# A fused Fourier mixer and gated MLP on one core: the last half sum of a seven-product block goes from a DMA to VectorE, the activation's addition and the second layer move one step later, and loads and buffers are rearranged

## The chip, the cores and the metric

The kernel runs on 1 core of one Trainium2 chip. The metric is the device time of one execution in microseconds (us), lower is better. Engines are named as the profile names them: PE is TensorE, PEld its weight loads, DVE is VectorE, ACT is ScalarE, POOL is GpSimd, SP is SyncE. POOL and SP issue the DMAs here.

## The reference

```python
# x (8, 3008, 256), filt_r and filt_i (1505, 256), w_in (256, 2048), w_out (2048, 256), alpha (2048)
X = np.fft.rfft(x, axis=1)
Y = X * (filt_r + 1j * filt_i)[None]
y = np.fft.irfft(Y, n=3008, axis=1).reshape(24064, 256)
h = y @ w_in
g = np.maximum(h, 0.0) + alpha * np.minimum(h, 0.0)
out = (g @ w_out).astype(np.float32)
```

So each of eight batches is filtered along its 3008 rows by a Fourier transform, and each of the 24064 rows then goes through a two-layer MLP with a leaky activation whose slope is given for each of 2048 hidden features.

## The kernel before, in words

**Two streams, one order.** Everything is issued in one hand-written order. The MLP works on 48 blocks of 512 rows (every twelfth, at n = 5 mod 12, has 384), and a block has 16 steps. In step j, `up(j)` multiplies the block's rows with 128 columns of `w_in` (two matmuls, L495). At every odd j the two hidden tiles just made are a pair: ACT copies the pair from PSUM to `gtb` (L503), DVE forms `m = min(g, 0) * (alpha - 1)` in two instructions (L506) and adds it to `g` (L507). The Fourier transform of batch b+1 runs beside the MLP of batch b in pieces named a, b, c, d; the tuples `STEPS_A` to `STEPS_D` (and `FIRST` for batches 1 to 3) say at which step, counted from p = 96(b-1), a piece is issued. `plan` holds these pieces, and each step runs its `plan` entries before `up(j)`.

**The second layer** of a block trails its first layer by `LAG` = 16 steps: after `up(j)`, items (matmuls) of the older block are issued as long as `done < (step - LAG) / 16`. For the 21 block numbers in `FAST`, the second layer is `seven()`: a 2 x 2 split with seven products instead of eight, 112 matmuls of 128 columns (L554), so seven a step. The four quarters of the block's `g` are `a11`, `a21`, `a12`, `a22`; the sums that the seven products need are made in halves h = 0, 1 by `sums(w, h)`:

- w = 1: `z1 = a21 + a22` on DVE (L515); w = 2: `z2 = z1 + a11` on DVE (L517)
- w = 3: `a21 += a11` by an accumulating DMA from POOL's queue (L519, rows `gtb<-gtb`)
- w = 4: `a12 += z2` by an accumulating DMA from POOL's queue (L521, rows `gtb<-ss`); it may start once the first product has read that half of `a12`, and the last product (items 96 to 111; its second half begins at item 104) reads the result

`SUMS` says at which step after a block's first one each sum is issued; `TAIL` does so for blocks 40 and 42 to 45. The other blocks use `eight()` (64 matmuls of 256 columns, L532).

**Around it.** Piece b takes one of two PSUM banks, DVE makes `ww` (L233) and `uu` (L234) from it, and two accumulating DMAs from POOL (L236, rows `uu<-ww`) finish `uu` for piece c (L248). `BANKS` is a string that says which of the two banks each piece gets. `load_x` brings a quarter c of a batch's rows in with two DMAs from POOL, one for each half (L168, `xs`). The results go out from `osb` tiles (pool `p_osb`, three buffers) by DMAs from SP's queue. `late` holds the last additions on DVE (L474) and the stores of a seven-product block, and `flush()` issues them at the start of the next step.

Of the kernel before, what the change touches and what calls it, by code (L numbers as in the profile page):

```python
# [10 lines left out]
FP16 = mybir.dt.float16  # L11
FP32 = mybir.dt.float32

NFFT = 3008
N1 = 47
N2 = 64
NK1 = 24
D = 256
# [2 lines left out]
NH = 32  # L21
BANKS = (
    "010101010101010101010101010101001010010110010010101010101010100101001010010101010101010100101010"
    "101010101010101010101001001010110100101010100101001000101101010101010101101001011101010001010010"
    "101101010011010101101010101010101010110010101010101101001000101001010101010101010101010101010110"
    "101010101011010010010101101010101010101010101010101010011010010101001011011101011010101010101010"
    "10101010101010010101010010110001010101010101010101010101"
)
STEPS_A = (-84, -81, -77, -76, -65, -59, -58, -58, -56, -53, -52, -51, -50, -48, -46, -43)
STEPS_B = (-21, -15, 4, 6, 13, 21, 25, 27, 32, 40, 54, 55)  # L30
# [5 lines left out]
STEPS_F = (20, 16, 22, 28, 34)  # L36
STEPS_K = (118, 121, 128, 133, 144)
STEPS_X = ((20, 27, 42, 52), (107, 109, 113, 126))
FIRST = (
# [12 lines left out]
)  # L52
FAST = frozenset((8, 10, 12, 14, 16, 18, 20, 22, 24, 26, 28, 30, 32, 34, 36, 38, 40, 42, 43, 44, 45))
SUMS = ((9, 1, 0), (10, 3, 0), (16, 2, 0), (17, 1, 1), (17, 3, 1), (19, 2, 1), (20, 4, 0), (21, 4, 1))
TAIL = ((12, 1, 0), (12, 3, 0), (18, 1, 1), (18, 3, 1), (18, 2, 0), (18, 2, 1), (20, 4, 0), (21, 4, 1))
LAG = 16
AF = mybir.ActivationFunctionType
OP = mybir.AluOpType

# [41 lines left out]
def kernel(  # L101
# [10 lines left out]
    nc = tc.nc  # L112
# [9 lines left out]
    konst = ctx.enter_context(tc.tile_pool(name="konst", bufs=1))  # L122
    p_x = ctx.enter_context(tc.tile_pool(name="p_x", bufs=4))
# [3 lines left out]
    p_sn = ctx.enter_context(tc.tile_pool(name="p_sn", bufs=1))  # L127
    p_uw = ctx.enter_context(tc.tile_pool(name="p_uw", bufs=3))
    p_m = ctx.enter_context(tc.tile_pool(name="p_m", bufs=2))
    p_osb = ctx.enter_context(tc.tile_pool(name="p_osb", bufs=3))  # L130
    psH = ctx.enter_context(tc.tile_pool(name="psH", bufs=2, space=bass.MemoryType.PSUM))
    psO = [ctx.enter_context(tc.tile_pool(name=f"psO{i}", bufs=1, space=bass.MemoryType.PSUM)) for i in range(2)]
    psF = [ctx.enter_context(tc.tile_pool(name=f"psF{i}", bufs=1, space=bass.MemoryType.PSUM)) for i in range(2)]
# [9 lines left out]
    twi_s = konst.tile([128, NK1, 128], FP16, name="twi_s")  # L143
    filt_s = konst.tile([128, NK1, D], FP16, name="filt_s")
    filts_s = konst.tile([128, NK1, D], FP16, name="filts_s")
    al16 = konst.tile([16, 128], FP32, name="al16")
    id32 = konst.tile([16, 16], FP32, name="id32")
    al_s = konst.tile([128, 16], FP32, name="al_s")
    alm_s = konst.tile([128, 16], FP32, name="alm_s")
# [11 lines left out]
    def xrow(b, h, c):  # L161
        return bass.AP(tensor=x.tensor, offset=x.offset + (b * NFFT + NH * h + 8 * c) * D,
                       ap=[[N2 * D, N1], [1, 8 * D]])

    def load_x(b, c):
        xs = p_x.tile([2 * N1, 8 * D], FP16, name="xs")
        for h in range(2):
            nc.gpsimd.dma_start(out=xs[h * N1 : h * N1 + N1], in_=xrow(b, h, c))  # L168
        return xs

    def load_filt(dst, pbase, src, ka, kb):
        n = kb - ka
# [181 lines left out]

    nc.sync.dma_start(out=id16, in_=id_d.ap())
    nc.sync.dma_start(out=wfx_s, in_=wfx_d.ap())
    xc = {(0, c): load_x(0, c) for c in range(4)}
    f0 = First()
    nc.sync.dma_start(out=al16, in_=moe_alpha.rearrange("(j p) -> j p", p=128))
    nc.sync.dma_start(out=wf1_s, in_=wf1_d.ap())  # L360
# [71 lines left out]
        for k in range(max(kp - 2, 0), kp - 1) if kp < 8 else (6, 7) if kp == 8 else (kp,):  # L432
            f0.piece_c(k, on_act)
    for c in range(4):
        xc[(1, c)] = load_x(1, c)
    for q in range(2):
        nc.gpsimd.dma_start(
            out=wout_s[:, 8 * q : 8 * q + 8],
            in_=moe_w_out[1024 * q : 1024 * q + 1024].rearrange("(j p) d -> p j d", p=128))
# [32 lines left out]
    def flush():  # L472
        for fn, args in late:
            fn(*args)  # L474
        late.clear()

    class Block:
# [12 lines left out]
        def up(self, j):  # L490
            tn = self.tn
            if j % 2 == 0:
                self.hps = psH.tile([128, 2, 512], FP32, name="hps")
            for kt in range(2):
                nc.tensor.matmul(self.hps[:, j % 2, 0:tn], win_s[:, kt, j * 128 : (j + 1) * 128],  # L495
                                 yT[:, kt, self.t0 : self.t0 + tn], start=(kt == 0), stop=(kt == 1))
            if j % 2 == 1:
                g = self.pair(j // 2)
                m = p_m.tile([128, 2, 512], FP16, name="m")
                hs, ms = self.hps[:, :, 0:tn], m[:, :, 0:tn]  # L500
                if self.fast:
                    hs, ms = (t.rearrange("p l (h c) -> p l h c", h=2) for t in (hs, ms))
                nc.scalar.activation(g, hs, AF.Copy)  # L503
                for i in range(2):
                    a = alm_s[:, j - 1 + i : j + i]
                    nc.vector.tensor_scalar(ms[:, i], g[:, i], 0.0, a, OP.min, OP.mult)  # L506
                nc.vector.tensor_add(g, g, ms)  # L507

        def sums(self, w, h):
            k = slice(4 * h, 4 * h + 4)  # L510
            a11, a21, a12, a22 = (self.q[:, l, t, k] for l in range(2) for t in range(2))
            z1, z2 = ss[:, 0, k], ss[:, 1, k]
            assert w != 4 or self.sent >= 8 * h + 8
            if w == 1:
                nc.vector.tensor_add(z1, a21, a22)  # L515
            elif w == 2:
                nc.vector.tensor_add(z2, z1, a11)  # L517
            elif w == 3:
                nc.gpsimd.dma_start(out=a21, in_=a11, accum_op=OP.add)  # L519
            else:  # L520
                nc.gpsimd.dma_start(out=a12, in_=z2, accum_op=OP.add)  # L521

        def items(self):
            return self.seven() if self.fast else self.eight()
# [87 lines left out]
    def put(step, fn, *args):  # L612
        plan.setdefault(step, []).append((fn, args))
# [17 lines left out]
    for b in range(1, NB):  # L631
        p = 96 * (b - 1)
        f = Fft(b)
        steps_a, steps_b, steps_c, steps_d = FIRST[b - 1] if b < 4 else (STEPS_A, STEPS_B, STEPS_C, STEPS_D)
        for i in range(16):
            put(p + steps_a[i], f.piece_a, i, on_act)
            if i % 4 == 3:
                put(p + steps_a[i] + (b > 2), f.save_a, i // 4)
        if b + 1 < NB:
            for c in range(4):  # L640
                put(STEPS_X[b - 1][c] if b < 3 else p - 8 + 4 * c,
                    lambda b=b, c=c: xc.update({(b + 1, c): load_x(b + 1, c)}))
        quarters, later = (4, 1) if b < 3 else (1, 4)
        w = NK1 // quarters
        for q in range(quarters):
            put(p + steps_a[15] + later, f.turn_a, nc.sync, w * q, w * q + w)
        for kp in range(12):
            put(p + steps_b[kp], f.piece_b, kp)
            put(p + steps_c[kp], f.piece_c, kp, on_act)
            if kp % 3 == 2:  # L650
                put(p + steps_c[kp] + 1, f.turn_c, kp // 3)
        for i in range(16):
            put(p + steps_d[i], f.piece_d, i, on_act)
        put(p + steps_d[3] + 2, f.load_z, 3)
# [15 lines left out]

    for n in range(5):
        put(STEPS_K[n], combine, n)
    blk, todo, ahead = Block(-2, 0, 0, 0), [], {}
    done = 0.0
    for n, (p, t0, tn, _) in enumerate(blocks):
        old, blk = blk, Block(n, p, t0, tn)
        if blk.fast:
            for at, w, h in SUMS if n < 39 and n - 1 not in FAST else TAIL:
                ahead.setdefault(16 * n + at, []).append((blk, w, h))
        for j in range(16):  # L680
            step = 16 * n + j
            flush()
            for b, w, h in ahead.pop(step, ()):
                assert w > 2 or not old.fast or b is old or old.sent >= 88 - 16 * w + 8 * h
                b.sums(w, h)
            for fn, args in plan.pop(step, ()):
                fn(*args)
            blk.up(j)
            while todo and done < (step - LAG) / 16:
                try:  # L690
                    done += next(todo[0])
                except StopIteration:
                    todo.pop(0)
        todo.append(blk.items())
    for it in todo[:-1]:
        for _ in it:
            pass
# [33 lines left out]
```

## Time and profile before

| What | Value |
|---|---|
| Median of 3 runs | 785.37 us (785.03 to 786.56) |
| The profiled execution's own time | 783.02 us |
| Its span, first to last instruction | 780.6 us |
| PE busy | 759.1 us, 97% |
| DVE busy | 687.2 us, 88% |
| ACT busy | 605.3 us, 78% |
| POOL busy | 277.3 us, 36% |
| Granted TensorE clock | 1.000 |

Busy time is time in which the profile shows the engine at an instruction. The ends of matmuls are modelled, so a PE that shows as busy can still run below its peak; its idle times and what ended them are the better guide. A row of the waits gives the engine and line that waited, what it waited for, the sum in us, the number of times, and the longest.

### The profile page before, as it was taken

The page shows a single profiled execution, that of the slowest core. Times are in us where ns is not written, and L with a number is a line of the kernel's source. Part 1 is how long each engine was busy: PE and PEld are TensorE (multiplying, and loading weights), DVE is VectorE, ACT ScalarE, POOL GpSimd, SP SyncE. Part 2 cuts the span into 40 slices and gives each one's busy share as a digit, 9 for nine tenths or more (in the row PEclk, how much of TensorE's full clock was granted, in tenths as well). Part 3 has the DMA queues.
Part 4 walks back from the last instruction along what each step waited for, and adds up shares of the span by engine and source line. Part 5 has one row for each costly group of instructions (what it writes and reads, how often), then busy time and mean ns, then how long its engine had stood idle before and what let it go on. Part 6 is the DMA issues. An engine that isn't in the chain of part 4 may idle for free. (4 is left out here: it accounts for less than half of the span.)

```text
span 780.6 us, 18307 instructions
## 1 busy us (share of the span) xinstructions
PE 759.1 (97%) x6952; PEld 540.0 (69%) x6952; DVE 687.2 (88%) x1501; ACT 605.3 (78%) x902; POOL 277.3 (36%) x367
## 2 busy tenths in 40 slices
PE   7899999999999999999999999999999999999998
PEld 6756667666667767676676766767667777777666
DVE  3788996899999899899898989889899999889994
ACT  3787778788778887788877887788878777787763
POOL 7830651245244351553334423434323434102210
PEclk9999999999999999999999999999999999999999
DMA  9996868667988679975888769886797555735642
GB/s 185 193 198 177 154 123 208 177 135 148 202 193 175 148 145 194 236 148 125 169 213 176 138 135 200 188 173 129 160 201 175 112 113 95 180 84 112 121 96 68
DMA packets 115184, 122.93 MB, mean 157 GB/s; under 512 B 12873, under 2 KB 94553, under 8 KB 115097
## 3 DMA queue, kind: packets, MB, share of 16 engines
q0 software_dynamic: 34960, 52.19, 41.0%
q1 hardware_dynamic: 79992, 69.52, 33.4%
q8 instruction: 54, 0.88, 0.5%
q14 instruction: 34, 0.27, 0.1%
q10 hardware_dynamic: 144, 0.07, 0.0%
HBM read 56.06 MB, written 46.66 MB: 132 GB/s over the span
## 5 line engine op out<-in xcount | busy, mean ns | idle before, releaser
L503 ACT ACTIVATE gtb<-hps 128x1024 f16<-128x1024 f32 (+1 forms) x384 | 386.4, 1006 | 106.9 <-PE hps L495 104.3
L495 PE MATMUL hps<-yT,win_s 128*128 128x512 f16 (+1 forms) x1536 | 449.3, 375 | 0.0
L506 DVE TENSOR_SCALAR m<-gtb,alm_s 128x512 f16<-128x512 f16 (+1 forms) x768 | 235.1, 348 | 52.3 <-ACT gtb L503 50.2
L507 DVE TENSOR_TENSOR gtb<-gtb,m 128x1024 f16<-128x1024 f16 (+1 forms) x384 | 261.5, 681 | 17.2
L532 PE MATMUL op<-wout_s,gtb 128*128 128x256 f16 x1600 | 243.3, 272 | 0.0
L532 PEld LDWEIGHTS <-gtb 128*128 128x128 f16 x1600 | 156.0, 98 | 105.1
L236 POOL DMA_DIRECT2D uu<-ww x168 | 141.7, 1041 | 242.7 <-DVE uu L234 131.2
L495 PEld LDWEIGHTS <-win_s 128*128 128x128 f16 x1536 | 136.6, 98 | 25.7 <-issue 2.6
L554 PEld LDWEIGHTS <-gtb 128*128 128x128 f16 x1680 | 114.4, 98 | 57.4 <-DMA gtb<-ss 5.0
L519 POOL DMA_DIRECT2D gtb<-gtb x42 | 41.5, 987 | 197.8 <-DVE ss L515 75.5
L554 PE MATMUL op<-wout_s,gtb 128*128 128x128 f16 x1008 | 85.8, 219 | 4.1 <-DMA gtb<-ss 3.6
L280 ACT ACTIVATE asb<-psF 96x512 f16<-96x512 f32 x112 | 65.4, 595 | 11.5 <-PE psF L210 10.8
L280 ACT ACTIVATE yT<-psF 128x376 f16<-128x376 f32 x120 | 57.3, 490 | 11.0 <-PE psF L273 10.4
L554 PEld LDWEIGHTS <-ss 128*128 128x128 f16 x672 | 47.1, 98 | 23.3
L554 PE MATMUL op<-tw_s,gtb 128*128 128x128 f16 x672 | 58.2, 219 | 0.1
L554 PE MATMUL op<-tw_s,ss 128*128 128x128 f16 x672 | 58.0, 219 | 0.0
L233 DVE TENSOR_TENSOR ww<-psF,filts_s 128x512 f16<-128x512 f32 x84 | 57.4, 683 | 0.0
L234 DVE TENSOR_TENSOR uu<-psF,filt_s 128x512 f16<-128x512 f32 x84 | 57.1, 679 | 0.0
L280 ACT ACTIVATE v<-psF 128x512 f16<-128x512 f32 x84 | 49.9, 599 | 9.1 <-PE psF L248 8.3
L168 POOL DMA_DIRECT2D xs<-in_x_dram x64 | 43.2, 1054 | 20.9 <-PE psF L210 13.5
L521 POOL DMA_DIRECT2D gtb<-ss x42 | 45.7, 1290 | 3.2 <-PE op L554 0.9
L210 PE MATMUL psF<-xs,wf_s 94*96 94x512 f16 x112 | 41.2, 381 | 1.8 <-DVE yT L283 0.5
(85 smaller groups left out, 518.2 us busy)
## 6 DMA issues: line engine op xcount, KB each, us to landing
out_dram<-osb SPq DMA_DIRECT2D x127, 128.0 KB
xs<-in_x_dram POOLq DMA_DIRECT2D x64, 188.0 KB, 7.0
a_dram<-asb SPq DMA_DIRECT2D x28, 384.0 KB
uu<-ww POOLq DMA_DIRECT2D x168, 64.0 KB, 3.2
v_dram<-v SPq DMA_DIRECT2D x112, 96.0 KB
zt<-v_dram SPq DMA_DIRECT2D x28, 384.0 KB
gtb<-gtb POOLq DMA_DIRECT2D x42, 256.0 KB, 4.2
gtb<-ss POOLq DMA_DIRECT2D x42, 256.0 KB, 6.1
```

The lines of the kernel that those rows point to most:

```text
L168: nc.gpsimd.dma_start(out=xs[h * N1 : h * N1 + N1], in_=xrow(b, h, c))
L233: nc.vector.tensor_mul(ww, px, filts_s[:, 2 * kp : 2 * kp + 2])
L234: nc.vector.tensor_mul(uu, px, filt_s[:, 2 * kp : 2 * kp + 2])
L236: nc.gpsimd.dma_start(out=uu[o : o + 64], in_=ww[64 - o : 128 - o], accum_op=OP.add)
L280: nc.scalar.activation(o, i, AF.Copy)
L495: nc.tensor.matmul(self.hps[:, j % 2, 0:tn], win_s[:, kt, j * 128 : (j + 1) * 128], yT[:, kt, self.t0 : self.t0 + tn], start=(kt == 0), st ...
L503: nc.scalar.activation(g, hs, AF.Copy)
L506: nc.vector.tensor_scalar(ms[:, i], g[:, i], 0.0, a, OP.min, OP.mult)
L507: nc.vector.tensor_add(g, g, ms)
L521: nc.gpsimd.dma_start(out=a12, in_=z2, accum_op=OP.add)
L532: nc.tensor.matmul(op[:, si % 2], self.pair(k // 2)[:, k % 2, 128 * si : 128 * si + 128], wout_s[:, k], start=(k == 0), stop=(k == 15))
L554: nc.tensor.matmul(acc[:, 128 * i : 128 * i + 128], x[:, k, 128 * i : 128 * i + 128], b[:, k], start=first and k + i == 0, stop=k == 7, sk ...
```

## The change

For seven-product blocks that follow `SUMS`, the sum w = 4, h = 1 becomes w = 6: the same addition, `a12 += z2` for the second half, as a DVE instruction at the same step 21 in place of the DMA. `TAIL` keeps its DMAs, and its first two sums move from step 12 to 13. The activation's addition is no longer issued in `up`: it is put into `owed` and issued by `settle()` in the next step, after that step's `flush`, sums and `plan` entries and before its `up`. `LAG` is 17, so the second layer comes a step later against the first. The loads of x for batches 4 to 7 are issued one half quarter at a time at `STEPS_Q`, from step p - 28 to p + 23, where they were issued two halves at a time at p - 8, p - 4, p and p + 4. `p_osb` has four buffers, and `al16` takes its space from one of them. `BANKS` differs in three of its five rows.

```diff
+STEPS_Q = (-28, -18, -8, -3, 1, 9, 15, 23)
...
-SUMS = ((9, 1, 0), (10, 3, 0), (16, 2, 0), (17, 1, 1), (17, 3, 1), (19, 2, 1), (20, 4, 0), (21, 4, 1))
-TAIL = ((12, 1, 0), (12, 3, 0), (18, 1, 1), (18, 3, 1), (18, 2, 0), (18, 2, 1), (20, 4, 0), (21, 4, 1))
-LAG = 16
+SUMS = ((9, 1, 0), (10, 3, 0), (16, 2, 0), (17, 1, 1), (17, 3, 1), (19, 2, 1), (20, 4, 0), (21, 6, 1))
+TAIL = ((13, 1, 0), (13, 3, 0), (18, 1, 1), (18, 3, 1), (18, 2, 0), (18, 2, 1), (20, 4, 0), (21, 4, 1))
+LAG = 17
...
-    p_osb = ctx.enter_context(tc.tile_pool(name="p_osb", bufs=3))
+    p_osb = ctx.enter_context(tc.tile_pool(name="p_osb", bufs=4))
...
-    al16 = konst.tile([16, 128], FP32, name="al16")
+    al16 = p_osb.tile([128, 2, D], FP32, name="osb")[0:16, 0, 0:128]
...
-    def load_x(b, c):
-        xs = p_x.tile([2 * N1, 8 * D], FP16, name="xs")
-        for h in range(2):
-            nc.gpsimd.dma_start(out=xs[h * N1 : h * N1 + N1], in_=xrow(b, h, c))
-        return xs
+    def load_x(b, c, halves=(0, 1)):
+        if 0 in halves:
+            xc[(b, c)] = p_x.tile([2 * N1, 8 * D], FP16, name="xs")
+        for h in halves:
+            nc.gpsimd.dma_start(out=xc[(b, c)][h * N1 : h * N1 + N1], in_=xrow(b, h, c))
...
-                nc.vector.tensor_add(g, g, ms)
+                owed.append((g, ms))
...
-            elif w == 3:
-                nc.gpsimd.dma_start(out=a21, in_=a11, accum_op=OP.add)
             else:
-                nc.gpsimd.dma_start(out=a12, in_=z2, accum_op=OP.add)
+                a, z = (a21, a11) if w % 2 else (a12, z2)
+                if w < 5:
+                    nc.gpsimd.dma_start(out=a, in_=z, accum_op=OP.add)
+                else:
+                    nc.vector.tensor_add(a, a, z)
...
-                put(STEPS_X[b - 1][c] if b < 3 else p - 8 + 4 * c,
-                    lambda b=b, c=c: xc.update({(b + 1, c): load_x(b + 1, c)}))
+                if b < 3:
+                    put(STEPS_X[b - 1][c], load_x, b + 1, c)
+                else:
+                    for h in range(2):
+                        put(p + STEPS_Q[2 * c + h], load_x, b + 1, c, (h,))
...
+    owed = []
+
+    def settle():
+        for g, ms in owed:
+            nc.vector.tensor_add(g, g, ms)
+        owed.clear()
+
...
             for fn, args in plan.pop(step, ()):
                 fn(*args)
+            settle()
             blk.up(j)
...
         todo.append(blk.items())
+    settle()
```

More of the change, by code (lines that the diff above doesn't have):

```diff
@@ L23 @@
     "010101010101010101010101010101001010010110010010101010101010100101001010010101010101010100101010"
-    "101010101010101010101001001010110100101010100101001000101101010101010101101001011101010001010010"
+    "101010101010101010101001010101001011010101011010110110101101010101010101101001011010101101010010"
     "101101010011010101101010101010101010110010101010101101001000101001010101010101010101010101010110"
-    "101010101011010010010101101010101010101010101010101010011010010101001011011101011010101010101010"
-    "10101010101010010101010010110001010101010101010101010101"
+    "101010101011010010010101101010101010101010101010101010010101101010110100100010100101010101010101"
+    "01010101010101101010101101001110101010101010101010101010"
 )
@@ L356 @@
     nc.sync.dma_start(out=wfx_s, in_=wfx_d.ap())
-    xc = {(0, c): load_x(0, c) for c in range(4)}
+    xc = {}
+    for c in range(4):
+        load_x(0, c)
     f0 = First()
@@ L434 @@
     for c in range(4):
-        xc[(1, c)] = load_x(1, c)
+        load_x(1, c)
     for q in range(2):
@@ L512, in sums @@
             z1, z2 = ss[:, 0, k], ss[:, 1, k]
-            assert w != 4 or self.sent >= 8 * h + 8
+            assert w not in (4, 6) or self.sent >= 8 * h + 8
             if w == 1:
@@ L684 @@
                 assert w > 2 or not old.fast or b is old or old.sent >= 88 - 16 * w + 8 * h
+                assert not (owed and b is blk and h == (j - 1) // 8)
                 b.sums(w, h)
```

## The prediction

> **What bounds the kernel now.** I read the page first, then the waits of PE and of its weight loads, then the same waits in short windows, and last the busy time of DVE for every two blocks. From the page:
>
> ```profile
> span 780.6 us, 18307 instructions
> PE 759.1 (97%) x6952; PEld 540.0 (69%) x6952; DVE 687.2 (88%) x1501; ACT 605.3 (78%) x902; POOL 277.3 (36%) x367
> ```
>
> PE is the bound: it stands idle for 780.6 - 759.1 = 21.5 us, and the change takes no matmul away. So all that it can win is in those 21.5 us (much of it before the first block begins at 37.5 us, and behind the last), and all that it can lose is new idle time of PE. Next, who ended PE's idle times (rows: waiter, what for, us in total, times, longest):
>
> ```profile
> PEld L554 <- DMA gtb<-ss: 5.0, 6, 1.4
> ...
> PEld L248 <- DMA uu<-ww: 2.6, 3, 1.1
> ...
> PEld L351 <- DVE uu L234: 0.9, 1, 0.9
> ...
> PEld L554 <- DVE gtb L507: 0.5, 2, 0.3
> ...
> PEld L554 <- DMA gtb<-gtb: 0.3, 1, 0.3
> ```
>
> The largest row is the last product of a seven-product block, which waits for the accumulating DMA into `a12`, the very DMA whose second half the change removes. I asked for the same rows in windows: 1.1 us in two waits from 215 to 232 us (block 10; the longer is 0.6), 0.9 in one from 314 to 331 (block 16), 1.4 in one from 405 to 420 (block 22), 1.0 in one from 500 to 512 (block 28), and 0.6 in one from 700 to 765 (block 43). Counting the 112 L554 matmuls of each block, PE stands at item 96 (half h = 0) for 0.6 in block 10 and 0.9 in block 16, and at item 104 (h = 1) for 0.5 in block 10, 1.4, 1.0 and the 0.6 of block 43. The 0.3 on `gtb<-gtb` is in block 10, the 0.5 on L507 in blocks 43 and 45. Why blocks 10, 16, 22 and 28? They are those with piece b at their steps 11 and 17 (p - 21 and p - 15). The timeline of POOL in block 28:
>
> ```profile
> 500.18 0.98 POOL L519 DMA_DIRECT2D gtb<-gtb  x1 [3.52 <-DVE ss L515]
> 501.38 1.66 POOL L236 DMA_DIRECT2D uu<-ww  x2 [0.22 <-issue]
> 502.44 2.54 POOL L521 DMA_DIRECT2D gtb<-ss  x2
> 503.62 5.27 POOL L168 DMA_DIRECT2D xs<-in_x_dram  x7
> ```
>
> POOL is in order: L521 stands behind L519, which waits for DVE's `z1`, and behind two `uu<-ww`, which wait for DVE's `ww` and `uu`. The issue comes 3.0 us after the matmuls of step 20 began (499.41), in blocks without that piece 0.5 us after. In block 28 that leaves 5.8 us to item 96 and 7.1 to item 104; L521 lands in 4.1 to 8.9 us, median 6.1. Last, DVE for each two blocks (columns: window, its length, DVE busy and instructions, clock, DMA share, GB/s):
>
> ```profile
> 480.40:510.20 29.80, 26.10 (x61) 1.00 0.95 207
> ...
> 632.20:661.40 29.20, 28.45 (x65) 1.00 0.57 109
> ...
> sum 575.10, DVE 528.18; mean DVE 27.80
> ```
>
> The mean window is 575.1 / 19 = 30.3 us, so DVE has 2.5 us free in it, but only 0.75 from 632 to 661 us, and that is no more than the pauses of 45 ns (17.2 us over 384) ahead of its 16 additions L507.
>
> **The change part by part.** Durations are of the profiled execution; its span is 780.6, its own time 783.02, which is 2.35 below the median of 785.37 that I forecast against. A step takes (768.9 - 37.5) / 768 = 0.95 us.
>
> *Second half sum on DVE.* 16 of the 21 seven-product blocks follow `SUMS`, so 16 DMAs leave POOL's queue and 16 additions of 128x1024 fp16 join DVE's. A sum of the same shape takes 0.685 us (L515, 28.8 / 42): 16 x 0.685 = 11.0 us more for DVE. It must wait until PE has sent 16 items, but DVE gets there later by itself: in block 28 item 16 ended at 499.3, while `z2`, which stands ahead of the sum, ended at 502.5. Behind it are the next pair's L506 and L507, read ten steps later, so nothing waits on it where DVE has room. It ends ten steps ahead of item 104: the waits there in blocks 10, 22 and 28 go, -2.9.
>
> *Second layer a step later (LAG).* Items 96 and 104 move 0.95 us away from the sums. Does the DMA for h = 0 move with them, since it must wait for item 8? No: in block 16 item 8 ended at 311.0 and the issue was at 315.4; in the tail, 703.6 against 707.1. So the 0.6 and 0.9 on h = 0, the 0.6 of block 43 and the 0.3 on `gtb<-gtb` are covered: -2.4. In block 16 the cover is 0.95 for 0.9, so I leave 0.3 of these waits in. At the start, step 17 loses four matmuls of 256 columns (0.44 us by the chain of waits) with which PE could fill waits for ACT: between 0 and +0.44, taken as +0.2, since PE there waits partly and partly not. At the end the last blocks have one step more of old items ahead of them: 0.
>
> *Addition a step later.* The order of DVE's instructions shows that 304 of the 384 additions still stand directly behind their own L506; 80 are passed: 33 by `ww` and `uu` (0.68 each), 15 by `z2` alone, 21 by one last addition of a seven-product block, 11 by others. Where nothing passes, LAG gives the reader 0.95 us more; where `z2` passes pair 7 of a fast block, 0.95 - 0.68 = +0.27 is left, and where `ww` and `uu` pass pair 7 (blocks 19, 25, 31, 37), 0.95 - 1.36 = -0.41 against a distance from that L507's end to PE's read of 1.6, 1.8, 1.2 and 1.3 us: enough. The smallest distances before are 0.05 to 0.25 us (blocks 16, 43, 45, 10, 40, 44) and become larger; the 0.5 on L507 goes: -0.5.
>
> *DVE's added load.* At 2.5 us free it costs nothing. From 601 to 661 us the additions of blocks 36 and 38, perhaps 34, fall where DVE has nothing free, and push all behind them by up to 3 x 0.685 = 2.0 us, against 0.95 us from LAG. Between 0 and +2.0; I take +0.7, one sum, as the distances of blocks 35 to 39 (0.9 to 2.5 us) cover the rest.
>
> *Loads of x.* The same 64 DMAs. POOL has 503.3 us free; no PE wait names `xs` after the first blocks. The eight loads jammed behind L521 held each other up (landing 7.0 to 10.8 us instead of 4.4 to 6.2), but not the sums ahead of them: h = 0 of block 28 landed in 4.53 with them, h = 1 of block 24 in 7.68 without. So their going is worth 0; up to -0.5 if they did slow the sums. What they now stand ahead of is a rival below.
>
> *Fourth result buffer, `al16`, `BANKS`.* ACT waits 0.4 us for a store and PE for none: 0. PE's waits on the two banks are under 5 us in sum, most of it before 92 us; a new order may win or lose 0.5: 0. Stores stand one step later in SP's queue, so some `v` and `zt` transfers go ahead of them; no PE wait names these: 0. The 1.6 us that L248 waits for `uu<-ww` at 486 us stays (its steps do not move), between -1.6 and 0.
>
> Sum: -2.9 - 2.4 - 0.5 + 0.3 + 0.2 + 0.7 = -4.6 us, so 785.4 - 4.6 = **780.8 us**, the profiled span near 776.0.
>
> **The rivals.**
>
> *No gain.* Only the waits at item 104 outside the tail go (-2.9); item 96 still waits because L521 lands late by more than a step gives (its landing varies by 4.8 us), DVE's load costs its full 2.0 and the start its 0.44: 784.9. Against it: the waits at item 96 are all under 0.95.
>
> *DVE becomes the bound (slower).* In 632 to 661 us it already is without free time. If that holds wherever the sums are added, PE waits for L507 by all of 11.0 us: 785.4 - 4.6 - 0.7 + 11.0 = 791.1. It decides where free time in two blocks is below 0.685 us. For it: 75% and more of the additions stay where they were, so the pauses of 45 ns stay too. Against it: 2.5 us are free in the mean.
>
> *Loads of x ahead of `uu<-ww`.* One half now goes out at p + 23, two steps before piece b at p + 25, in the same queue. A `uu<-ww` that was issued some 2.1 us behind two halves (at 168.9 and 169.5) landed in 5.5 and 6.0 us; piece c had 7.4, 6.0, 6.2 and 5.6 us from that issue in batches 3 to 6. At 6.0 that is 0.4 us once: 781.2. At the 7.8 us of the slow row at 222.9 it is 0.4 + 1.8 + 1.6 + 2.2 = 6.0: 786.8. The Trainium skill ("DMA: Bandwidth & Descriptors", "Queues, rings and completion order") says that on each DMA engine the descriptors of a ring are taken in ring order; by that rule it is what stands ahead that delays, which speaks for this rival, and against any gain from taking the loads away behind the sums. The 4.53 us of block 28 agree.
>
> **How the numbers follow.** The forecast has 0.62 (its own range 777 to 783.8). More than that, with the 1.6 at L248 and 0.5 each from loads and banks gone too and no new cost, 776.5 or below: 0.06. No gain 0.12, all of it within 0.2%. DVE as the bound 0.12, slower. The loads ahead of `uu<-ww` 0.08, shared 0.02, 0.03, 0.03 over faster, same and slower. A measurement of this kernel can tell about 0.2% (1.6 us) from no change, so faster is 0.70, same 0.15, slower 0.15. The range of 776.5 to 787.0 takes in the second end of the loads and the no-gain case; it leaves out DVE as the bound and half of the best case, with a little of each edge: under 0.2.
>
> **What would show it.** Right: no PEld wait on `gtb<-ss` from 180 to 660 us, or under 0.5 us in sum; 16 DVE additions `gtb<-gtb,ss` near 0.685 us; 26 rows `gtb<-ss`; DVE near 698 us busy; PE idle near 17 us. Wrong: rows PEld L554 or L532 waiting for DVE's addition by over 2 us, above all from 600 to 690 us (DVE the bound); L248 waiting for `uu<-ww` near 355, 450 and 540 us (loads ahead); a longer stretch before 90 us.

## The result, and the profile after

The changed kernel takes 778.88 us (median of 4 runs, 778.49 to 781.17) against 785.2 us of the kernel before (4 runs, 782.83 to 786.56): a ratio of 0.9937, 95% interval 0.9911 to 0.9963. By the medians it is faster by 6.3 us where 4.6 were forecast; by the ratio it is 4.9 us, and the interval spans 2.9 to 7.0. The profiled execution took 778.49 us.

The page after, first its head:

```profile
span 776.7 us, 18287 instructions
PE 759.6 (98%) x6952; PEld 541.9 (70%) x6952; DVE 691.0 (89%) x1517; ACT 606.1 (78%) x902; POOL 264.7 (34%) x351
```

PE's idle time fell from 21.5 to 17.1 us with the same 6952 matmuls. The span fell by only 3.9 us, less than the medians: the first matmul of step 0 began at 38.8 us here and at 37.5 before. That is not the change: `late_spread` below has the same start and begins it at 37.2; in this execution the granted clock was 0.91 from 20 to 40 us, before it was 1.00. From the first to the last step it is 725.8 us against 731.4, so 5.6 less. What follows took 0.4 us more, since the lag leaves one step more of the second layer there. The waits of the weight loads (what waited, for what, us in total, times, longest) show which went:

```profile
PEld L559 <- DMA gtb<-ss: 1.0, 2, 0.8
PEld L249 <- DMA uu<-ww: 0.9, 1, 0.9
PEld L352 <- DVE uu L235: 0.8, 1, 0.8
...
PEld L559 <- DVE gtb L685: 0.6, 1, 0.6
```

(L559, L249, L352 and L685 are L554, L248, L351 and L507 of before.) The wait for the sum fell from 5.0 to 1.0, that of piece c for `uu<-ww` from 2.6 to 0.9, and the 0.3 for `gtb<-gtb` is gone; the 0.5 on the activation's addition left blocks 43 and 45, but 0.6 came up in block 8. Together -4.0 - 1.7 - 0.3 + 0.1 = -5.9, about the 5.6; smaller rows moved both ways. DVE's two-block windows (window, length, DVE busy and instructions, clock, DMA share, GB/s):

```profile
478.20:506.80 28.60, 25.82 (x61) 1.00 1.00 216
...
628.90:658.00 29.10, 28.48 (x64) 1.00 0.50 99
...
sum 570.50, DVE 532.58; mean DVE 28.03
```

A window has 570.5 / 19 = 30.0 us, so 2.0 us are free instead of 2.5, and 0.6 instead of 0.75 in the second one shown. The 16 new additions took 0.684 us each. And the queue of POOL in block 28, whose `gtb<-ss` is now alone but lands late (in 6.6 us; item 96 could start only 6.7 us after the issue, 0.8 of them a wait of PE):

```profile
492.16 1.14 POOL L170 DMA_DIRECT2D xs<-in_x_dram  x1
496.53 0.97 POOL L524 DMA_DIRECT2D gtb<-gtb  x1 [3.23 <-PE op L559]
498.95 1.65 POOL L237 DMA_DIRECT2D uu<-ww  x2 [1.46 <-DVE ss L520]
500.01 1.51 POOL L524 DMA_DIRECT2D gtb<-ss  x1
500.59 2.54 POOL L170 DMA_DIRECT2D xs<-in_x_dram  x3
```

The first line is the half at p - 18, now ahead of the sums.

### The profile page after: what moved, and what is told of

It reads as the page before. It is cut to its first block, busy times and chain, and to the rows that moved or that the text cites. A ratio compares the mean times of both kernels' runs of the same rounds, so it can differ in the third digit from the quotient of the medians.

```text
span 776.7 us, 18287 instructions
## 1 busy us (share of the span) xinstructions
PE 759.6 (98%) x6952; PEld 541.9 (70%) x6952; DVE 691.0 (89%) x1517; ACT 606.1 (78%) x902; POOL 264.7 (34%) x351
## 4 chain that ended last, share of the span: by engine, by line
PE 87%; DVE 4%; DMA 4%; ACT 3%; issue 1%; POOL 1%; SPq 1%; DVEq 0%; ACTq 0%; POOLq 0%
PE hps L498 38%; PE op L537 20%; PE op L559 16%; PE psF L211 3%; PE psF L274 3%; PE psF L249 2%; PE psF L231 2%; ACT gtb L506 2%; DMA twf_s<-c_twf 1%; DVE m L509 1%; DVE gtb L685 1%; DMA zt<-v_dram 1%; PE op L592 1%; DVE ww L234 1%; DVE uu L235 1%
## 5 line engine op out<-in xcount | busy, mean ns | idle before, releaser
L506 ACT ACTIVATE gtb<-hps 128x1024 f16<-128x1024 f32 (+1 forms) x384 | 385.9, 1005 | 110.5 <-PE hps L498 106.5
L685 DVE TENSOR_TENSOR gtb<-gtb,m 128x1024 f16<-128x1024 f16 (+1 forms) x384 | 260.9, 679 | 14.2
L537 PE MATMUL op<-wout_s,gtb 128*128 128x256 f16 x1600 | 243.1, 272 | 0.0
L537 PEld LDWEIGHTS <-gtb 128*128 128x128 f16 x1600 | 156.0, 98 | 104.6
L559 PEld LDWEIGHTS <-gtb 128*128 128x128 f16 x1680 | 114.3, 98 | 53.8 <-DMA gtb<-ss 1.0
L559 PE MATMUL op<-wout_s,gtb 128*128 128x128 f16 x1008 | 85.1, 219 | 1.1 <-ACT gtb L506 0.6
L559 PEld LDWEIGHTS <-ss 128*128 128x128 f16 x672 | 47.1, 98 | 23.3
L170 POOL DMA_DIRECT2D xs<-in_x_dram x64 | 54.4, 1014 | 14.2 <-PE psF L211 13.4
L559 PE MATMUL op<-tw_s,gtb 128*128 128x128 f16 x672 | 58.1, 219 | 0.0
L559 PE MATMUL op<-tw_s,ss 128*128 128x128 f16 x672 | 58.0, 219 | 0.0
L274 PE MATMUL psF<-wi_s,zt 96*128 96x94 f16 x504 | 39.4, 205 | 2.2 <-ACT yT L281 1.4
```

The source lines that it names most:

```text
L274: nc.tensor.matmul(ps[:, m], self.zt[g][:, 4 * mh + m, dh * 128 : dh * 128 + 128], wi3_s, start=True, stop=True)
L537: nc.tensor.matmul(op[:, si % 2], self.pair(k // 2)[:, k % 2, 128 * si : 128 * si + 128], wout_s[:, k], start=(k == 0), stop=(k == 15))
L559: nc.tensor.matmul(acc[:, 128 * i : 128 * i + 128], x[:, k, 128 * i : 128 * i + 128], b[:, k], start=first and k + i == 0, stop=k == 7, sk ...
```

## The experiments

Ratios are to the kernel before, measured beside each group on the same chip; it had medians of 784.27 us beside the first four kernels, 785.87 beside the next four and 784.6 beside the last four. The kernel after was measured for the result above alone. So a difference from it is one of medians from two groups, between which the kernel before differs by up to 1.6 us, and a small one counts only where a trace shows it. Each kernel is one of the two, or `without_spread` below, with the edit shown.

### The sum alone, and the lag alone

```diff
 # only_sum: the kernel before, with
-... (20, 4, 0), (21, 4, 1))
+... (20, 4, 0), (21, 6, 1))
```

> The kernel before with one edit: the second half of the last sum on VectorE (w = 6 in place of the DMA), LAG 16. Theory A (the prediction: the sum takes the waits at item 104 of blocks 10, 22 and 28, the lag takes those at item 96 and in the tail): 2.9 us faster, no wait at item 104 between 180 and 660 us, those at item 96 (0.6 and 0.9 us) still there. Rival B (the lag alone takes nearly all waits, the sum is hardly needed): also 2.9 us faster, since without the lag the sum is the only cure. Rival C (VectorE is the bound): slower by up to 11 us, waits of PE on the activation's addition.

782.53 us, ratio 0.9976 (0.9959 to 0.9993). No wait at item 104 from 180 to 660 us; the two at item 96 were there, 1.4 and 1.2 us in this run. Theory A's mechanism holds; VectorE as the bound (rival C) falls. The gain of 1.9 us (0.5 to 3.2 by the interval) can't be told from 2.9. New in this execution is a wait of 1.9 us for a bank that ACT empties, up to 684 us; ACT stood there for 2.3 us at a result tile that a store still held. The third buffer can thus be missing without the lag too.

```diff
 # only_lag: the kernel before, with
-LAG = 16
+LAG = 17
```

(and the first two sums of `TAIL` at 13.)

> The kernel before with LAG 17 and the first two sums of TAIL at 13, nothing else. Theory A: the waits of 0.6, 0.9, 0.6, 0.3 and 0.5 us go, and each of the three at item 104 loses up to 0.95 us: 2.9 us from the first five and 0.5 + 0.95 + 0.95 = 2.4 from the others, 5.3 us faster before 0.2 us lost at the start. Rival B: the same 5.3 us, and then the kernel after without the sum must be as fast as the kernel after. Rival D (the DMA moves with the lag because it waits for the product that reads its target): under 2 us faster, the waits on gtb<-ss stay near 5 us.

782.92 us, ratio 0.9984 (0.9966 to 1.0002): no clear gain, where 5.3 us were expected. But of PEld on `gtb<-ss` only 0.2 us is left of 5.0, so rival D falls, and the lag alone does remove the waits that theory A and rival B name. It brings other waits, of PE and of ACT:

```profile
PE op L554 <- DVE osb L474: 2.1, 3, 0.8
```

```profile
ACT osb L568 <- DMA out_dram<-osb: 2.6, 1, 2.6
PEld L554 <- issue: 1.1, 1, 1.1
...
PE op L554 <- ACT osb L568: 0.9, 1, 0.9
```

The first view is the waits of PE, the second the waits of all engines from 316 to 320.5 us. The three waits on L474 are in blocks 43 to 45, of 0.85, 0.51 and 0.78 us. DVE's timeline shows the first:

```profile
717.06 0.61 DVE L506 TENSOR_SCALAR m<-gtb,alm_s 128x512 f16<-128x512 f16 x2
717.78 0.69 DVE L507 TENSOR_TENSOR gtb<-gtb,m 128x1024 f16<-128x1024 f16 x1
718.39 0.68 DVE L474 TENSOR_TENSOR osb<-op,osb 128x512 f32<-128x512 f32 x1
```

L474 reads the PSUM bank into which the next block's second product goes. With LAG 16 it was issued at an odd step, ahead of that step's pair; with 17 it is issued at an even step, behind the L506 and L507 of the pair just made, and PE's next matmul began at 719.12. The other wait is of ACT for a free result buffer, and PE for ACT.

### The change without the sum, and without the lag

```diff
 # without_sum: the kernel after, with
-... (20, 4, 0), (21, 6, 1))
+... (20, 4, 0), (21, 4, 1))
```

> The kernel after with the second half sum back as a DMA. Theory A: at item 104 of blocks 22 and 28 0.4 and 0.1 us of wait are left behind the lag, and VectorE is free of 11 us of work: within 1 us of the kernel after, either way. Rival E (what is gained beyond the removed waits comes from fewer accumulating DMAs in the queue of POOL): 2 us or more slower than the kernel after, with waits on gtb<-ss and uu<-ww back.

784.91 us, ratio 1.0000 (0.9982 to 1.0018): the whole gain is gone, and of rival E's two rows the one on `gtb<-ss` is there; none on `uu<-ww` is in this window. The waits of the weight loads from 180 to 660 us:

```profile
PEld L559 <- DMA gtb<-ss: 7.1, 8, 1.7
...
PEld L559 <- DMA gtb<-gtb: 1.3, 2, 1.0
```

That is more than in the kernel before, in spite of the lag. In block 22 the two DMAs landed in 8.6 and 9.1 us, where the lag alone had 4.8 and 7.7. So something else in the change makes these DMAs slow, and the sum on VectorE takes one of the two out of its way. Rival B is open for a kernel without that something else: the lag alone left 0.2 us of these waits, and no run has all of the change but the sum and the spread of the loads, so what the sum is worth there is not shown.

```diff
 # without_lag: the kernel after, with
-LAG = 17
+LAG = 16
```

(and `TAIL` as before.)

> The kernel after with LAG 16 and TAIL's first sums at 12. The addition still comes a step later, so its distance to PE's read falls by 0.95 us. Theory A: where nothing passes the addition the waits are those of before at item 96 (1.5 us), in the tail (0.6 and 0.5) and on gtb<-gtb (0.3); pair 7 of the seven-product blocks, passed by z2 (0.68), had 0.05 to 1.35 us and now waits in some ten blocks for up to 0.6 us: 4 to 8 us slower than the kernel after, with a row PEld on the activation's addition of 3 us or more. Rival F (the lag matters only for the waits on DMAs): 2.5 to 3.5 us slower, that row under 1 us.

784.34 us, ratio 0.9990 (0.9971 to 1.0009); from 180 to 765 us:

```profile
PEld L559 <- DMA gtb<-ss: 3.2, 3, 1.6
PEld L559 <- DVE gtb L685: 2.9, 6, 1.5
```

5.5 us slower than the kernel after, as theory A said, on both rows that it named (with 0.7 us more on the addition in L537). The later addition has no room without the lag; rival F falls.

### The loads, the buffer, the later addition, the bank string

```diff
 # without_spread: the kernel after, with
-                if b < 3:
-                    put(STEPS_X[b - 1][c], load_x, b + 1, c)
-                else:
-                    for h in range(2):
-                        put(p + STEPS_Q[2 * c + h], load_x, b + 1, c, (h,))
+                put(STEPS_X[b - 1][c] if b < 3 else p - 8 + 4 * c, load_x, b + 1, c)
```

> The kernel after with the loads of x for batches 4 to 7 at p - 8 + 4c again, both halves at once. In the kernel after, L524's sum for h = 0 in blocks 16, 22 and 28 lands in 7.1, 8.6 and 6.7 us, in the kernel before in 6.0, 6.4 and 4.5. Theory A (as in the prediction: the spread is worth nothing, and halves ahead in the ring slow what stands behind): these landings fall to about those of before, the 0.8 us wait of block 28 goes, time within 1 us of the kernel after. Rival G (the spread is a good part of the gain, since eight loads at once jam POOL and the DMA engines): 1.5 us or more slower than the kernel after, with waits on gtb<-ss or uu<-ww that the kernel after does not have.

776.73 us (775.73 to 777.58), ratio 0.9874 (0.9843 to 0.9906). This is faster than the kernel after by 2.1 us, and no run of the one reaches a run of the other. `gtb<-ss` in block 22 lands in 5.6 us, and no PEld row on `gtb<-ss` is left. Rival G falls: the spread costs time. Of the 1.9 us between the two profiled spans, 1.0 lies between the first and the last step, which is the 1.0 on `gtb<-ss`; 0.8 is an earlier start, which the edit does not touch. ACT waits for a store in neither of the two kernels by more than 0.2 us.

```diff
 # three_bufs: the kernel after, with
-    p_osb = ctx.enter_context(tc.tile_pool(name="p_osb", bufs=4))
+    p_osb = ctx.enter_context(tc.tile_pool(name="p_osb", bufs=3))
```

(and `al16` in `konst`.)

> The kernel after with three result buffers and al16 in a place of its own. The prediction said 0 for the buffer. The lag alone showed ACT waiting 2.6 us at 316 us for a store before it could evict, and PE 1.1 us for ACT. Theory H (with the lag a fourth buffer is needed): that wait of PE on ACT's osb is back near 318 us, 1 us or more slower than the kernel after. Rival I (the fourth buffer only moves stores forward in SP's queue and so onto the accumulating DMAs): landings of gtb<-ss in blocks 16, 22 and 28 fall below those of the kernel after, and the time is the same or less.

786.67 us, ratio 1.0002 (0.9970 to 1.0034): one buffer less, and in the median all of the gain is gone. The 12 runs go from 780.61 to 794.37 us; the profiled one took 790.73, so its waits are above the usual. From 300 to 520 us:

```profile
ACT osb L573 <- DMA out_dram<-osb: 13.7, 3, 5.9
```

(L573 is L568 of before.) ACT stands for up to 5.9 us at a result tile, and all evictions behind it in its queue stand too; PE then waits for banks (its row on ACT's `yT`: 10.0 us in 6, the longest 4.7). From 40 us on the granted clock was below 1.00 only where PE stood for the two longest of these waits and right behind them, at the least 0.78 from 410 to 415 us and 0.50 from 510 to 515, which adds to their cost. Theory H holds, by far more than its 1 us.

```diff
 # without_settle: the kernel after, with
-                owed.append((g, ms))
+                nc.vector.tensor_add(g, g, ms)
```

> The kernel after with the activation's addition at once in up, as before. The lag alone showed PE waiting 1.0, 0.7 and 0.9 us in blocks 43 to 45 for the last addition of the block ahead (osb<-op,osb), which stood behind a pair's addition. Theory J (the addition is moved a step so that this last addition stands ahead of it): those three waits are back, and PE's waits on bank evictions by ww and uu grow; 2 to 3 us slower than the kernel after. Rival K (as the prediction had it: nothing but the order of 80 additions, no wait depends on it): within 0.8 us of the kernel after, PE's waits on L479 under 0.5 us.

782.76 us, ratio 0.9952 (0.9928 to 0.9977), so 3.9 us slower than the kernel after by the medians, and 1.2 by the ratios, whose intervals overlap; by the traces it is 4.5 us longer from the first to the last step. PE's waits from 700 to 765 us:

```profile
PE op L559 <- DVE osb L477: 2.1, 3, 0.8
```

The same three waits as with the lag alone (L477 is L474 of before). Theory J holds on them: with the addition a step later a block's last addition stands ahead of it. The longer waits on bank evictions that it named did not come. A wait for `gtb<-ss` of 2.0 us in block 28, where the kernel after has 0.8, is 1.2 us of the rest; why it is longer is not shown.

```diff
 # old_banks: the kernel after, with the five rows of BANKS of the kernel before
```

> The kernel after with the bank string of before. The prediction gave it 0 with 0.5 us either way. Theory L: PE's waits on the two banks (psF rows that name ACT or DVE) stay within 0.5 us of the kernel after. Rival M (the string is fitted to the new order and is part of the gain): those waits grow by 1.5 us or more, and the time with them.

779.5 us, ratio 0.9923 (0.9894 to 0.9952): as the kernel after, and the `psF` waits on ACT and DVE are within 0.5 us of it. Rival M falls; the string is worth nothing that these runs can tell.

### What made the sums land late, and when VectorE binds

```diff
 # late_spread: the kernel after, with
-STEPS_Q = (-28, -18, -8, -3, 1, 9, 15, 23)
+STEPS_Q = (-11, -8, -5, -2, 1, 9, 15, 23)
```

> The kernel after with STEPS_Q = (-11, -8, -5, -2, 1, 9, 15, 23): the two halves that stood at p - 28 and p - 18, ahead of the sum at p - 12, go behind it; the last four stay spread. Theory N (a half of x at p - 18 takes the DMA engines' time ahead of the sums of blocks 16, 22 and 28, which then land late): their landings for h = 0 fall to those of the kernel without the spread (5.1, 5.6, 4.4 us), no wait of PE there, 776 to 778 us where the kernel after has 779. Rival O (the sums land late because halves are issued one by one among the uu<-ww, wherever they stand): landings stay at 6.7 to 8.6 us and the time at that of the kernel after.

776.87 us (775.42 to 777.85), ratio 0.9896 (0.9874 to 0.9919). `gtb<-ss` in blocks 16, 22 and 28 lands in 5.1, 5.5 and 4.4 us, with 7.1, 8.6 and 6.6 in the kernel after. POOL's rows in block 22, first of the kernel after, then of this one:

```profile
399.47 1.15 POOL L170 DMA_DIRECT2D xs<-in_x_dram  x1
403.84 1.00 POOL L524 DMA_DIRECT2D gtb<-gtb  x1 [3.23 <-PE op L559]
404.80 1.89 POOL L237 DMA_DIRECT2D uu<-ww  x2
405.86 1.76 POOL L524 DMA_DIRECT2D gtb<-ss  x1
406.47 2.85 POOL L170 DMA_DIRECT2D xs<-in_x_dram  x3
```

```profile
401.64 1.02 POOL L524 DMA_DIRECT2D gtb<-gtb  x1 [3.77 <-PE op L559]
402.61 1.89 POOL L237 DMA_DIRECT2D uu<-ww  x2
403.67 1.75 POOL L524 DMA_DIRECT2D gtb<-ss  x1
404.25 3.88 POOL L170 DMA_DIRECT2D xs<-in_x_dram  x5
```

The queue at the sum is the same but for the one half ahead, and five halves behind do no harm. Theory N holds in its landings and its time. Both early halves were moved, so that it is the one at p - 18 rests on its place only.

How does a half that is issued 6.4 us ahead do it? What the DMA queues moved in block 22 from 2 us before the sum's issue to 2 us after it (packets, MB, share of the 16 engines; q0 is POOL's queue, q1 is SP's), first in the kernel after, then in this one:

```profile
q1 hardware_dynamic: 419, 1.08, 96.4%
q0 software_dynamic: 3, 0.01, 0.8%
```

```profile
q1 hardware_dynamic: 594, 0.70, 56.8%
q0 software_dynamic: 241, 0.34, 49.9%
```

In the kernel after POOL's queue all but stands still, with the sum and three DMAs ahead of it issued, while SP's queue fills the engines. In blocks 16 and 28 POOL's queue moves 0.06 and 0.25 MB in such a stretch, with 0.39 and 0.47 here. Its traffic is three `zt` loads of 384 KB and the stores behind them. The `zt` loads go out 5.5, 4.9 and 6.3 us ahead of the sum in blocks 16, 22 and 28 of the kernel after, and 8.7, 7.3 and 8.5 us ahead here. So the traces say that the half ahead makes the `zt` loads late, and that these then meet the sum. That is read from three blocks; no run moves the `zt` loads alone. `late_spread` and `without_spread` are the two fastest kernels of this study and can't be told apart.

```diff
 # spreadless_three_bufs: without_spread, with
-    p_osb = ctx.enter_context(tc.tile_pool(name="p_osb", bufs=4))
+    p_osb = ctx.enter_context(tc.tile_pool(name="p_osb", bufs=3))
```

> The kernel without the spread (776.7 us) and with three result buffers. Theory P (with the lag the stores are issued about 1.5 us later behind the zt loads, so a third buffer is not free in time, whatever the loads of x do): ACT waits for stores in blocks 16, 22 and 28 by 2 us or more in sum, 2 to 8 us slower than without the spread alone. Rival Q (it was the half at p - 18 that made the stores late): ACT's wait under 1 us, time within 1 us of the kernel without the spread.

777.4 us, ratio 0.9909 (0.9885 to 0.9933): within 1 us of `without_spread`, and ACT waits once, 1.4 us, at a store. Rival Q holds by the time, though its wait was to be under 1 us; theory P falls: it is the spread that makes the stores late. That its early halves do it, through the `zt` loads ahead of the stores in SP's queue, is likely but not shown, as no run has `late_spread` with three buffers. The fourth buffer is worth under 1 us without the spread and over 5 us with it, by the medians, so in the change one edit repairs what another breaks.

```diff
 # two_more_sums: without_spread, with two more additions at step 22 that nobody reads
-... (20, 4, 0), (21, 6, 1))
+... (20, 4, 0), (21, 6, 1), (22, 8, 1))
...
+            if w == 8:
+                m = p_m.tile([128, 2, 512], FP16, name="m").rearrange("p a (b c) -> p (a b) c", b=2)
+                for _ in range(2):
+                    nc.vector.tensor_add(m, a22, ss[:, 1, k])
+                return
```

> The kernel without the spread with two further VectorE additions of 128x1024 per SUMS block, at step 22, whose result nobody reads: 32 x 0.685 = 21.9 us more of VectorE. Theory A (VectorE has room): 2.5 - 0.7 = 1.8 us are free in two blocks and 1.37 are taken, so under 1 us in most blocks and 1 to 4 us in all, nearly all of it after 590 us, as waits of PE on the activation's addition. Rival R (VectorE is already the bound): 15 us or more slower. Rival S (there is room everywhere): under 0.5 us.

784.64 us, ratio 1.0000 (0.9986 to 1.0013). None of the three sizes: 21.9 us more of work cost 7.9 us, over 1 to 4 and under 15. Nor is the place what theory A said. PE's waits from 180 to 660 us:

```profile
PE psF L274 <- DVE uu L235: 3.9, 5, 1.0
PE psF L211 <- DVE uu L235: 1.0, 1, 1.0
...
PE op L564 <- DVE gtb L686: 0.5, 1, 0.5
```

(L564 and L686 are L559 and L685 of the kernel after.) PE waits for a PSUM bank that `ww` and `uu` have not read yet, hardly for the activation's addition. These bank rows are 4.9 of the 7.9 us; 1.2 more are waits on `gtb<-ss` in block 40. So DVE binds mostly through the bank it holds, at 0.36 us for each further us at this place of the order, while its windows of two blocks still show 1.5 us free in the mean.

```diff
 # lag_sum_bufs: the kernel before, with LAG 17 and TAIL at 13, the sum w = 6, four result buffers
```

> The kernel before with three edits: the sum on VectorE, LAG 17 with TAIL at 13, four result buffers. Not in it: the addition a step later, the spread, the new bank string. Theory T (these three make the gain, and the spread costs 2 us and the later addition wins 3): waits of PE on the last additions in blocks 43 to 45 of 2.6 us, few others, 777 to 781 us against 785 for the kernel before. Rival U (the edits only work all together): no better than the lag or the sum alone, 782 us or more.

780.23 us, ratio 0.9942 (0.9920 to 0.9963): three edits reach what the whole change reaches (0.9937). PE waits 2.1 us on L474, three times in blocks 43 to 45, where theory T said 2.6; rival U falls. With the later addition and the string, but no spread, it is 776.73.

## Why the prediction was right, and where it was not

The sign, the size to within 1.9 us and the main cause hold: PE was bound by waits that an accumulating DMA ended, and most of them went. That the size came so close is in part luck: costs that the sum lacks (the spread, the stores, the last additions) were hidden or made up for by edits that it priced near 0, and by a wait that it left in. The sign of under 0.5 us on `gtb<-ss` was not met (1.0). By its steps:

- **The sum on DVE, -2.9.** Right: no wait at item 104 in blocks 10, 22 and 28, though the lag alone takes these waits too. The sum took 0.684 us where 0.685 was put.
- **The lag, -2.4 with 0.3 left.** The waits on `gtb<-gtb`, in block 43 and in block 10 went; 1.0 was left on `gtb<-ss` instead of 0.3 (0.2 in block 16, and 0.8 in block 28, where none was at item 96 before). It was mis-sized because the landing was taken as unchanged, and the early halves made it later (4.4 us in block 28 with them moved, 6.6 in the change).
- **"At the end ... 0" and the stores "0".** Wrong for the lag by itself: it moves each block's last addition behind a pair's L506 and L507 and the stores to where a third buffer is not always free, and it leaves 0.4 us more behind the last step. The first two costs were hidden by two edits that the prediction put at 0 or near it: **the later addition** (-0.5; it is worth 3.9 us by the medians, 2.1 of them in the three waits) and **the fourth buffer** (0; over 5 us in this change). The order of DVE had shown that 21 last additions now pass L507; the step that failed was to price this passing by what the passed addition loses and not by what the passing one wins.
- **Later addition, smallest distances grow.** Right in blocks 10, 16, 40 and 43 to 45 (0.4 to 1.0 us after). The lag makes them grow, and the later addition takes some of it back (0.85 to 1.3 us in `without_settle`). Wrong in block 8: a weight sum, `ww`, `uu` and `z2` pass pair 7 there and PE waits 0.6.
- **DVE's load, +0.7.** No row of PE in 590 to 690 us names it; the free time in two blocks fell by 0.5. The bound is nearer than the prediction thought, as the two further sums showed, and lies mostly at the banks.
- **Loads of x, 0.** Wrong: the spread costs 2.0 to 2.1 us by the medians, 1.0 to 1.9 by the traces from the first to the last step. The reason given, that loads behind a sum do not slow it, held (5.5 us with five behind). (The jammed loads landed in 6.8 us at least, not 7.0.) The rival of loads ahead was right in kind and looked in the wrong place, at p + 23 ahead of `uu<-ww`, where no wait came; the half that does harm is ahead of the sums. The rule of the Trainium skill ("DMA: Bandwidth & Descriptors", "Queues, rings and completion order") that a ring is taken in order agrees with both. But the half ahead had landed at 404.2 us by the trace, 1.7 us before the sum's issue, so ring order alone does not explain the delay. The same page of the Trainium skill ("Issuing engines are not separate DMA queues") says that DMAs of all issuing engines run on the same 16 DMA engines. The trace agrees: SP's queue had 96.4% of the engines around that issue and POOL's 0.8%. A busy engine alone is not it, for the DMA share from 404 to 408 us is 0.99 in the kernel after and 1.08 in `without_spread`, where the sum landed in 5.6 us; what differs is whose traffic fills them.
- **L248's 1.6 us at 486, "stays".** Wrong: it went. With the lag alone it is still 1.6 us, with the sum alone 0.2, and with all of the change but the sum it is gone too, so more than one edit takes it away. The first of the four `uu<-ww` was issued 9.4 us ahead of piece c before, and they landed in 4.2 to 9.0 us; in the kernel after it is 11.0 us, and they land in 2.5 to 4.5. Which edit does how much of this is open. The 1.6 us are most of the 1.7 us by which the medians are better than the forecast, but that difference is within the interval.
- **`BANKS`, 0.** Right.
- **DVE near 698 us busy.** It was 691.0: the additions take 10.9, but instructions with no wait between them start 0.61 us apart at 0.69 us each (as the rows of DVE with the lag alone show), and the later addition makes more of these: without it (`without_settle`) DVE is busy for 694.9 us.

## What to carry to other kernels

When a step in an in-order schedule is moved, list what now stands ahead of what in every queue, and price each passing from both sides; here the lag flipped a last addition behind a pair on VectorE, and the 2.1 us of waits that came were nearly the 2.4 that the lag was to remove. In this kernel a transfer whose arrival ends a wait was slowed by a load issued ahead of it, and not by loads issued behind it, so bulk loads belong behind it; and the load did it by way of another queue, so look at what every queue moves around the issue. And an edit that is worth little beside one set of edits (a buffer, without the spread) can be all of the gain beside another: take parts out one by one from the changed kernel as well as adding them to the old one.

## What was not expected of the hardware

One load of 188 KB issued 6.4 to 7.9 us ahead of an accumulating DMA of 256 KB went with landings later by 2.0, 3.1 and 2.2 us in three blocks, though it had landed itself before the sum was issued. In the 4 us around the issue in block 22 POOL's queue moved 0.01 MB beside 1.08 MB of SP's, though four of its DMAs were issued: here a burst of one queue held up the other almost fully. And two further additions for each of 16 blocks cost PE 0.36 us for each us of VectorE while VectorE's windows of two blocks still showed free time, mostly because what it delays is the release of one of two banks. In the kernel with three buffers the granted clock was 0.50 from 510 to 515 us, where a wait of PE of 4.7 us ended; around one of 1.9 us, near 318 us, it stayed at 1.00.
